# Attention and expert layer on one core: a v load ahead of a weight load, batch 1's and batch 2's loads in later slots

## The chip, the cores and the metric

The kernel runs on one core of one Trainium2 chip. The metric is the device time of one execution in microseconds; the time before is the median of four runs. A core has five engines that run side by side, each in its own order: TensorE (PE in the profile, its weight loads PEld), VectorE (DVE), ScalarE (ACT), GpSimd (POOL) and SyncE (SP, which here only issues DMAs).

## The reference

Sliding-window attention with a linear bias, followed by a two-layer network with an ELU between its layers. Sizes: 8 batches, 8 heads, 576 positions, 64 values a head; 4608 tokens of width 512, inner width 2048.

```python
scores = scale * np.matmul(q, k.transpose(0, 1, 3, 2))
rel = pos[:, None] - pos[None, :]
bias = slopes[:, None, None] * (-np.abs(rel))[None, :, :]
mask = (rel >= 0) & (rel < window)            # window = 128
scores = np.where(mask, scores + bias[None], -1000000000.0)
attn = np.exp(scores - np.max(scores, axis=-1, keepdims=True))
attn = attn / (np.sum(attn, axis=-1, keepdims=True) + 1e-09)
x = np.matmul(attn, v)                        # tokens x 512 after a transpose
h = x @ w_in
g = np.where(h > 0.0, h, np.exp(np.minimum(h, 0.0)) - 1.0)
out = g @ w_out
```

All inputs and the output are float32 in memory; the DMAs that load q, k, v, w_in and w_out turn them into float16 on the way.

## The kernel before

The program is written out in one order by hand: the order of the Python calls is the order of each engine's instructions, and the framework adds only the waits. After a start that is written line by line (L327 to L385) everything hangs on numbered **slots**. Three tables say what a slot holds: `HID[s]` the step of the first layer, `OUT[s]` four matmuls of the second, and `at(s, f, ...)` adds any other call (`before` puts it at the head of the slot, `after` at its end). The loop at L517 walks the slots.

One step of the first layer (`hidden`, L272) is 16 matmuls (L280, 32 in the steps of 64 tokens) into a PSUM buffer of 512 columns, an exp on ScalarE (L285), a clamp to 0..1 on POOL (L286), and one slot later `elu` on VectorE (L293), which reads the PSUM buffer again and so sets it free. Up to slot 17 three buffers take turns from slot 4 on, so a step waits for the elu of the step three before it. Steps 0 to 15 make the first 512 tokens; slots 18 to 23 hold no step.

The attention of batch 0 is spread over slots 0 to 12, that of batch 1 over slots 16 to 32, that of batch 2 over 32 to 48, and so on. A query block's `values` (L235) multiplies weights and v on TensorE (L245), then VectorE takes the reciprocal of the row sums (L251) and scales (L252) into `xn`; `turn` (L255) transposes xn on TensorE (L264) and copies it into `xT`, what the first layer reads.

Loads. q and k of batches 0 and 1 are loaded by `load_first` (L96) in parts and transposed on TensorE by `turn_first` (L125, matmuls L134, copies L138). q and k of later batches come by `load_qk` (L103), eight loads a batch, and are transposed on VectorE by `turn_qk` (L140, L142), whose first call for K needs all four K loads. `load_v` (L110) loads 128 positions of v (five a batch) into one of two buffers, `load_wi` and `load_wo` a quarter of a weight. **All of these are issued on POOL's queue**, in the same order as POOL's clamps: a load that stands in slot s is issued after the clamp of step s and ahead of that of step s+1. An issue shows as a POOL row of about 0.7 to 0.9 us (DMA_DIRECT2D). The stores (L307) are issued on SP.

What the change touches: the start's loads (L330 to L339), the list of batch 1's loads (L460 to L465), the first turn of K of batch 2 (`TURN`, L486), and the slots of batch 2's loads (L512, L514). In the start TensorE works through 22 warming matmuls (L321), K and Q of batch 0, two query blocks and their turns; step 0 (slot 0) is its first use of w_in, and `values(0, 1, ...)` its first use of v's second piece.

Of the kernel before, what the change touches and what calls it, by code (L numbers as in the profile page):

```python
# [18 lines left out]
def kernel(  # L19
# [76 lines left out]
    def load_first(b, w, part):  # L96

        p0, n, m, r0, j0 = split(b, w, part)
        nc.gpsimd.dma_start(
            s0[b][p0:p0 + n, w, :, j0:j0 + m, :].rearrange("p h j d -> p h (j d)"),  # L100
            (q, k)[w][b, :, r0:r0 + n * m, :].rearrange("h (p j) d -> p h (j d)", j=m))
# [8 lines left out]
    def load_v(b, n):  # L110
        p = 128 if n < 4 else 64
        nc.gpsimd.dma_start(VP[b % 2][0:p, n, :, 0:D],  # L112
                            v[b, :, 128 * n:128 * n + p, :].rearrange("h p d -> p h d"))

    def load_wi(i):
        c = slice(512 * i, 512 * i + 512)
        nc.gpsimd.dma_start(w_in_sb[:, :, c], moe_w_in[:, c].rearrange("(c p) f -> p c f", p=128))
# [28 lines left out]
    with tc.manual_schedule():  # L146
# [182 lines left out]
        nc.gpsimd.iota(rel, pattern=[[1, 256]], base=0, channel_multiplier=-1)  # L329
        load_first(0, 0, 0)  # L330
        load_v(0, 0)
        load_wi(0)
        load_v(0, 1)
        load_first(0, 0, 1)
        load_first(0, 1, 1)
        load_first(0, 0, 2)
# [53 lines left out]
        def at(s, f, *a):  # L390
            tasks.setdefault(s, []).append((f, a))

        def after(s, f, *a):
            late.setdefault(s, []).append((f, a))

        def before(s, f, *a):
            early.setdefault(s, []).append((f, a))
# [15 lines left out]
        for o in range(16 * NTB - 4):  # L413
            t, ts, f = o // 16, o // 4 % 4, o % 4
            s = (9, 11, 13, 14)[o] if o < 4 else 11 + o if o < 13 else 2 * o - 1 if o < 16 else 15 + o
# [42 lines left out]
        for n in range(4):  # L458
            at(n + 1, load_wo, n)
        at(5, load_first, 1, 1, 0)  # L460
        at(6, load_first, 1, 0, 0)
        at(9, load_first, 1, 1, 1)
        at(10, load_first, 1, 0, 1)
        for n, s in enumerate((7, 8, 11, 12, 13)):
            at(s, load_v, 1, n)  # L465
        at(16, turn_first, 1, 1, 0, 0, av, V.tensor_copy)
        at(16, turn_first, 1, 1, 0, 1, sp[3], nc.scalar.copy)
# [15 lines left out]

        START = [None, None, 32, 49, 66, 83, 100, 117]

        TURN = [None, None, (20, 22, 23, 24, 24, 25, 27, 29), (40, 40, 41, 42, 44, 44, 46, 48)]  # L486
        REST = 32, 32, 36, 36, 33, 34, 37, 38
        for b in range(2, B):
            for u in range(4):
                a = START[b] + 4 * u  # L490
                after(a, scores, b, u)
                for g in range(4):
                    before(a + 1 + g // 2, expo, b, u, g)
                at(a + 1, weigh, b, u, 0)
                at(a + 2, weigh, b, u, 1)
                at(a + 3, values, b, u, 0, sp[2])
                at(a + 3, values, b, u, 1, sp[3])
                at(a + 3, turn, b, u)
                if u == 3:
                    at(a + 4, values, b, 4, 0, sp[0])  # L500
                    at(a + 4, values, b, 4, 1, sp[2])
                    at(a + 4, turn, b, 4)
            a = START[b - 1] if b > 2 else 0
            for n in range(8):
                piece = (b, int(n < 4), *divmod(n % 4, 2))
                if b == 2:
                    m = 4 if n < 4 else 6
                    at(TURN[b][n], turn_qk, *piece, 0, m)
                    at(REST[n], turn_qk, *piece, m, R)
                else:  # L510
                    at(TURN[b][n] if b == 3 else a + 4 * (n // 2), turn_qk, *piece)
                at(a - 8 + n if a else 14 + n // 2, load_qk, b, int(n < 4), n % 4)  # L512
            for n in range(5):
                at(a + 3 + n if a else 18 + n // 2, load_v, b, n)  # L514

        slots = set(HID) | set(OUT) | set(tasks) | set(early)
        for s in range(min(slots), max(slots) + 1):  # L517
# [42 lines left out]
```

## Time and profile before

| | |
|---|---|
| median of four runs | 319.15 us |
| the runs | 318.97, 319.46, 319.32, 318.7 us |
| the profiled execution | 318.97 us |
| its span, first to last instruction | 317.2 us |
| mean granted TensorE clock | 0.999 |
| DMA queue of POOL | 75920 packets, 18.36 MB, 64.2% of 16 engines' span |

```profile
DMA  9999999895999999993969697996912111120011
```

The line above cuts the span into 40 slices of 7.9 us; each digit is the share of a slice, in tenths, in which the DMA engines are busy on average. The other views used here: the waits (who waited for whom, how long in total, how often, the longest), the chain of waits (the work that ended last, followed back), the timeline (start, length, engine, line, operation; in brackets the engine's idle time before it and what ended it), and a tile's rows, which also give the time from a load's issue to its landing. Times in them count from the start of the span.

### The profile page before, as it was taken

The numbers are of one execution on the slowest core, as the hardware profiler recorded it, in microseconds if no ns is written. First come the engines' busy times: TensorE is split into PE (matmuls) and PEld (weight loads), VectorE is DVE, ScalarE is ACT, GpSimd is POOL, SyncE is SP. The second block draws the span as 40 slices with busy tenths as digits, with TensorE's granted clock in tenths as the row PEclk, the third lists the DMA queues.
The fourth block names the chain that finished last, engine by engine and source line by source line (L and its number), as shares of the span: only waits on it lengthen the run. The fifth ranks groups of instructions, "written<-read, shape, count | busy, mean of one in ns | idle before, by whom it ended". The sixth has DMA issues, their size and how long they took to land.

```text
span 317.2 us, 9362 instructions
## 1 busy us (share of the span) xinstructions
PE 310.9 (98%) x3935; PEld 220.0 (69%) x3935; DVE 218.9 (69%) x444; ACT 179.9 (57%) x320; POOL 169.3 (53%) x263
## 2 busy tenths in 40 slices
PE   8899999999999999999999999999999999999996
PEld 6788774787777777776667666666677666766653
DVE  4646657887898877787777777777886666644330
ACT  5575458666666465546566666656654666533431
POOL 8949887473756455564756375645623323333320
PEclk9999999999999999999999999999999999999999
DMA  9999999895999999993969697996912111120011
GB/s 103 194 193 206 198 174 185 96 117 74 100 81 115 112 69 110 121 118 61 114 98 124 95 100 94 124 121 78 98 52 60 36 50 53 52 58 35 33 65 70
DMA packets 96362, 32.00 MB, mean 101 GB/s; under 512 B 83904, under 2 KB 91840, under 8 KB 96320
## 3 DMA queue, kind: packets, MB, share of 16 engines
q0 software_dynamic: 75920, 18.36, 64.2%
q1 hardware_dynamic: 20400, 13.05, 16.8%
q8 instruction: 31, 0.51, 0.7%
q14 instruction: 11, 0.09, 0.1%
HBM read 36.70 MB, written 9.44 MB: 145 GB/s over the span
## 4 chain that ended last, share of the span: by engine, by line
PE 93%; DVE 4%; POOL 1%; issue 1%; ACT 0%; ACTq 0%; DVEq 0%
PE hp L280 38%; PE op L299 20%; PE av L299 16%; PE spa L222 4%; PE sp L245 4%; PE op L321 2%; DVE g L293 1%; PE sp L299 1%; DVE xn L252 1%; PE sp L280 1%; PE av L313 1%; POOL e L286 1%; PE spa L173 1%; PE av L134 1%; PE av L245 1%
## 5 line engine op out<-in xcount | busy, mean ns | idle before, releaser
L286 POOL TENSOR_SCALAR e<-e 128x512 f32<-128x512 f32 x144 | 90.0, 625 | 134.4 <-ACT e L285 133.9
L280 PEld LDWEIGHTS <-wi 128*128 128x128 f16 x1856 | 124.5, 98 | 34.9 <-issue 4.6
L280 PE MATMUL hp<-xT,wi 128*128 128x128 f16 (+2 forms) x1744 | 144.9, 233 | 0.6 <-DVE g L293 0.3
L285 ACT ACTIVATE e<-hp 128x512 f32<-128x512 f32 x138 | 82.7, 599 | 86.2 <-PE hp L280 83.0
L293 DVE SCALAR_TENSOR_TENSOR g<-e,hp 128x512 f16<-128x512 f32 x138 | 94.2, 682 | 53.6 <-POOL e L286 52.6
L299 PE MATMUL op<-wo,g 128*128 128x512 f16 x304 | 77.5, 379 | 0.0
L299 PEld LDWEIGHTS <-g 128*128 128x128 f16 x560 | 50.1, 98 | 36.8 <-issue 1.1
L299 PE MATMUL av<-wo,g 128*128 128x512 f16 x240 | 61.4, 379 | 0.0
L233 DVE TENSOR_TENSOR EX<-EX,TAB 128x1024 f16<-128x1024 f16 x48 | 33.1, 690 | 15.0 <-ACT EX L228 14.8
L228 ACT ACTIVATE EX<-spa 128x512 f16<-128x512 f32 x48 | 26.1, 594 | 16.4 <-PE spa L222 16.4
L112 POOL DMA_DIRECT2D VP<-in_v_dram x40 | 34.9, 874 | 0.4 <-issue 0.2
L252 DVE TENSOR_TENSOR xn<-sp,rden 128x256 f16<-128x256 f32 (+1 forms) x60 | 25.4, 424 | 2.1
L228 ACT ACTIVATE EX<-sp 128x512 f16<-128x512 f32 x48 | 26.1, 600 | 0.0
L245 PEld LDWEIGHTS <-EX 128*128 128x128 f16 x576 | 22.3, 97 | 2.4 <-DVE EX L213 1.1
L142 DVE STREAM_TRANSPOSE QT<-st 128x576 f16<-128x576 f16 (+2 forms) x28 | 19.1, 714 | 0.0
L245 PE MATMUL sp<-VP,EX 128*128 128x65 f16 x428 | 18.9, 193 | 0.0
L142 DVE STREAM_TRANSPOSE KT<-st 128x576 f16<-128x576 f16 (+2 forms) x28 | 18.8, 710 | 0.0
L106 POOL DMA_DIRECT2D st<-in_k_dram x24 | 16.5, 687 | 1.2 <-DMA VP<-in_v_dram 0.4
L306 ACT COPY ob<-op 128x512 f32<-128x512 f32 x19 | 11.1, 586 | 9.4 <-PE op L299 9.1
L106 POOL DMA_DIRECT2D st<-in_q_dram x24 | 16.4, 684 | 0.0
L222 PEld LDWEIGHTS <-KT 32*128 32x128 f16 x480 | 8.9, 93 | 10.4 <-issue 10.2
L222 PE MATMUL spa<-QT,KT 32*128 32x256 f16 (+2 forms) x240 | 14.7, 248 | 0.0
(108 smaller groups left out, 188.3 us busy)
## 6 DMA issues: line engine op xcount, KB each, us to landing
out_dram<-ob SPq DMA_DIRECT2D x35, 256.0 KB, 2.3
VP<-in_v_dram POOLq DMA_DIRECT2D x32, 128.0 KB, 4.4
st<-in_k_dram POOLq DMA_DIRECT2D x24, 144.0 KB, 3.5
st<-in_q_dram POOLq DMA_DIRECT2D x24, 144.0 KB, 3.8
wi<-in_moe_w_in_dram POOLq DMA_DIRECT2D x4, 512.0 KB, 10.6
wo<-in_moe_w_out_dram POOLq DMA_DIRECT2D x4, 512.0 KB, 10.2
VP<-in_v_dram POOLq DMA_DIRECT2D x8, 64.0 KB, 4.6
s<-in_k_dram POOLq DMA_DIRECT2D x1, 512.0 KB, 12.0
```

The source lines that it names most:

```text
L106: nc.gpsimd.dma_start(st[b][32 * g:32 * g + 32, w, :, :, :, :].rearrange("p h n j d -> p (h n) (j d)"), (q, k)[w][b, 2 * g:2 * g + 2, :, : ...
L112: nc.gpsimd.dma_start(VP[b % 2][0:p, n, :, 0:D], v[b, :, 128 * n:128 * n + p, :].rearrange("h p d -> p h d"))
L142: V.transpose(o, st[b][:, w, h2, n0:n1, :, 32 * dh:32 * dh + 32])
L222: nc.tensor.matmul(sp[g][:, 256 * h2 + o:256 * h2 + o + n], kt_[b % 2][r, k0:k0 + 128], QT[b % 2][r, h2, dh, q0:q0 + n], start=dh == 0, st ...
L228: nc.scalar.activation(unit(b, u)[:, g, :, :], sp[g].rearrange("p (h c) -> p h c", h=2), AF.Exp, scale=0.125)
L233: V.tensor_tensor(out=e, in0=e, in1=TAB[:, int(u == 3), 2 * gp:2 * gp + 2, :, :], op=ALU.mult)
L245: nc.tensor.matmul(a[:, x, h2, :], ex_[u][:, c:c + 128], VP[b % 2][:, n, 2 * g + h2, 0:D + 1], start=j == 0, stop=j == len(parts) - 1)
L280: nc.tensor.matmul(p[:, l * w + u0:l * w + u1], w_in_sb[:, c, fc * 128:(fc + 1) * 128], xT[:, c, x0:x0 + u1 - u0], start=(c == 0), stop=(c ...
L285: nc.scalar.activation(e[:, 0:n], p[:, 0:n], AF.Exp)
L286: nc.gpsimd.tensor_scalar(out=e[:, 0:n], in0=e[:, 0:n], scalar1=1.0, scalar2=0.0, op0=ALU.min, op1=ALU.max)
L293: V.scalar_tensor_tensor(out=gs[t][:, f0:f0 + nf, c0:c0 + w], in0=sh(es.pop((t, c0, f0))), scalar=1.0, in1=sh(hps.pop((t, c0, f0))), op0=A ...
L299: nc.tensor.matmul(o, gs[t][:, fc, ts * 128:(ts + 1) * 128], w_out_sb[:, fc, :], start=(fc == 0), stop=(fc == NFC - 1))
```

## The change

Four edits, all of them to the order of loads; the arithmetic stays.

1. In the start, v's second piece (128 positions of batch 0) is loaded before w_in's first quarter instead of after it.
2. Batch 1: k's main part stays in slot 5; q's main part goes from slot 6 to 9, the rest of k from 9 to 11, the rest of q from 10 to 12, v's five pieces from 7, 8, 11, 12, 13 to 10, 11, 13, 14, 15.
3. Batch 2: the eight q and k loads go from slots 14 to 17 to slots 16 to 19, two a slot as before, the five v loads from 18 to 20 to slots 20 to 22.
4. Batch 2's first turn of K goes from slot 20 to 21.

```diff
         load_first(0, 0, 0)
         load_v(0, 0)
+        load_v(0, 1)
         load_wi(0)
-        load_v(0, 1)
         load_first(0, 0, 1)
...
         at(5, load_first, 1, 1, 0)
-        at(6, load_first, 1, 0, 0)
-        at(9, load_first, 1, 1, 1)
-        at(10, load_first, 1, 0, 1)
-        for n, s in enumerate((7, 8, 11, 12, 13)):
+        at(9, load_first, 1, 0, 0)
+        at(11, load_first, 1, 1, 1)
+        at(12, load_first, 1, 0, 1)
+        for n, s in enumerate((10, 11, 13, 14, 15)):
             at(s, load_v, 1, n)
...
-        TURN = [None, None, (20, 22, 23, 24, 24, 25, 27, 29), (40, 40, 41, 42, 44, 44, 46, 48)]
+        TURN = [None, None, (21, 22, 23, 24, 24, 25, 27, 29), (40, 40, 41, 42, 44, 44, 46, 48)]
...
-                at(a - 8 + n if a else 14 + n // 2, load_qk, b, int(n < 4), n % 4)
+                at(a - 8 + n if a else 16 + n // 2, load_qk, b, int(n < 4), n % 4)
             for n in range(5):
-                at(a + 3 + n if a else 18 + n // 2, load_v, b, n)
+                at(a + 3 + n if a else 20 + n // 2, load_v, b, n)
```

## The prediction, made before the changed kernel ran

> **What bounds the kernel now.** I read the busy shares first, then the waits of TensorE, then the chain of work through the one stretch where TensorE waits twice, then the rows of that stretch engine by engine.
>
> ```profile
> PE 310.9 (98%) x3935; PEld 220.0 (69%) x3935; DVE 218.9 (69%) x444; ACT 179.9 (57%) x320; POOL 169.3 (53%) x263
> ```
>
> TensorE is busy 310.9 of 317.2 us, so the change can win only what TensorE waits for. Its waits over 0.15 us (engine, line and what it waited for; total, times, longest) are few, the start-up wait for the warming operand left out:
>
> ```profile
> PE hp L280 <- DVE g L293: 0.3, 1, 0.3
> PE hp L264 <- DVE xn L252: 0.3, 1, 0.3
> PE av L245 <- DVE xn L252: 0.3, 1, 0.3
> PE op L264 <- DVE xn L252: 0.2, 1, 0.2
> ```
>
> By the timeline, L264's two lie at 11.68 and 13.81 us (the start), L280's at 28.77 and L245's at 32.37. The chain of waits (start, length, what) shows what stands behind the last one:
>
> ```profile
> 27.39 0.60 POOL e L286
> 28.00 0.87 POOL s L99
> 28.87 0.04 issue
> 28.90 0.63 POOL e L286
> 29.53 0.85 POOL VP L112
> 30.38 0.04 issue
> 30.42 0.64 POOL e L286
> 31.05 0.02 issue
> 31.08 0.69 DVE g L293
> ...
> 32.92 0.38 PE sp L264 x4
> ```
>
> This is the place to look at. From 27.39 to 31.06 the chain lies on POOL, and two of its five pieces are not arithmetic but the issuing of DMAs: batch 1's q (slot 6, 0.87 us) and its first v piece (slot 7, 0.85 us). They hold up the clamps (L286) of steps 7 and 8, these the elu (L293), and VectorE, which works in order, gets to the reciprocal and xn of query block 3 only then. TensorE's side of it:
>
> ```profile
> 28.77 1.05 PE L280 MATMUL hp<-xT,wi 128*128 128x128 f16 x16 [0.32 <-DVE g L293]
> ...
> 31.01 1.06 PE L280 MATMUL sp<-xT,wi 128*128 128x128 f16 x16
> 32.37 0.40 PE L245 MATMUL av<-VP,EX 128*128 128x65 f16 x8 [0.30 <-DVE xn L252]
> 32.92 0.38 PE L264 MATMUL sp<-ident,xn 128*128 128x128 f16 x4
> 33.14 1.06 PE L280 MATMUL hp<-xT,wi 128*128 128x128 f16 x16
> ```
>
> A row of matmuls ends on the page some 0.16 us (1.05 - 0.89) after the last could be followed by another, so the loss is read from starts. The same 16 matmuls of L280 are followed at 29.66 after a start at 28.77: 0.89 us. From 31.01 that is 31.90, but L245 starts at 32.37: **0.47 us** lost. Eight matmuls of L245 without a wait take 29.66 to 29.90, 0.24; from 32.37 that is 32.61, but L264 starts at 32.92: **0.31 us** lost. Together 0.78. From 33.14 to the end hardly more than switches between shapes (about 0.1 us each) is lost before a matmul.
>
> **Part 1, batch 1's q and v leave slots 6 to 8.** Removed between the clamps there are three issues, 0.92 us each on their rows. The new POOL order is worked out from the exp rows, which feed the clamps:
> - Clamp 6 stays at 27.39: it waited for its exp (26.70 + 0.60), with POOL idle for 0.58 us after batch 1's first k load. So elu 6 (28.03) stays, and TensorE's stall at 28.77, which ends with elu 6 at 28.72, **stays whole**.
> - Clamp 7: its exp ends at 27.59 + 0.60 = 28.19; start 28.28 instead of 28.90 (0.09 from exp to clamp, as at step 6). Clamp 8: exp ends 29.08, start 29.17 instead of 30.42. Clamp 9: exp ends 30.46, start 30.55 instead of 31.93.
> - Elu 8 begins 0.03 us after clamp 8's 0.60: 29.80 instead of 31.08. Block 3's first half is then held by TensorE (L245 at 29.66 + 0.41 = 30.07) and elu 8 (the next row starts 0.60 after it, as from 31.08 to 31.68: 30.40): reciprocal 30.40, xn 30.61 to 31.03; second half reciprocal 30.95, xn 31.16 to 31.58.
> - TensorE wants the first at 31.90 and the second at 32.14. Both are ready, by 0.9 and 0.6 us. So both losses go: **-0.78 us**, and L280 of step 11 starts at 32.36.
>
> I take the whole 0.78. Bounds: no gain at all if some other input holds those two rows; at the most 1.27, with the 28.77 stall gone too (0.49: from 27.39 + 0.89 = 28.28 to 28.77), which the exp rows above speak against.
>
> **Part 2, where these issues go.** Everything below is 0.78 earlier than its row. q (0.92) behind clamp 9 ends at 32.0; clamp 10 waits for its exp to 32.70 anyway. v's first (0.92) behind clamp 10 ends at 34.3, clamp 11's exp at 34.1: late by 0.15. Slot 11 gets two issues (0.71 + 0.92): clamp 12 starts near 36.5 instead of 36.15. The buffer of step 12 is wanted by step 15 (row at 39.88, new 39.10), elu 12 ends at 37.8: 1.3 us to spare. Slots 13 to 15 have one issue each, as 11 to 13 had. Slots 14 and 15 lose one of their two, and with them the waits of the batch 2 loads (0.33, 0.16, 0.38 and 0.30 us in the POOL rows from 40.85 to 44.38). Cost **0**: hidden by the 1.3 us of buffer slack; with that gone, 0.15 to 0.35 us would show.
>
> Do the loads still come in time? They stay in one order of issue but for k's rest and v's second piece, and the backlog sets the landings (a tile's rows give the time from issue to landing: 12.6 us for the issue at 27.95): q still near 40.6 for its turn at 44.8; q's rest near 44.7 (row: 33.79 + 10.9) for its turn at 48.1; v's first near 41.5 for L245 at 49.5. Each load also waits for the eighth before it to land (the load at 40.85 starts just after q's 27.95 + 12.6 = 40.55); later issue makes this wait shorter. Cost **0**.
>
> **Part 3, batch 2 two slots later.** K's last quarter is issued in slot 17 behind clamp 17, whose exp ends at 46.29, new 45.51: second issue at 46.8 instead of 44.38. The landing of the old row, and the VectorE rows around the first turn's new place (slot 21):
>
> ```profile
> DMA to landing us min/median/max: 6.1/6.1/6.1
> ```
> ```profile
> 52.81 0.68 DVE L213 TENSOR_TENSOR EX<-EX,TAB 128x1024 f16<-128x1024 f16 x1
> 54.02 0.18 DVE L251 RECIPROCAL rden<-sp 128x4 f32<-128x4 f32 x1 [0.52 <-PE sp L245]
> ```
>
> The old landing is 44.38 + 6.1 = 50.5. The new one lies between 46.8 + 3.1 = 49.9 (the load at 58.83, with an empty queue, takes 3.1) and 46.8 + 7.0 = 53.8 (the load at 40.85, with a full one). I take about 50.5, as the same bytes lie ahead of it. The turn can start when L213 lets it, 53.41 - 0.78 = 52.6: 2 us to spare. Its 0.46 us lies in VectorE's 0.52 of idle time before 54.02, where slot 20 had it between 51.78 and 52.24. Cost **0**; at 53.8 VectorE would stand from 52.6 on and TensorE's L245 (55.31, which waits for the next L213) would be some 0.9 late.
>
> [...]
>
> **Part 4, v's second piece before w_in's first quarter.** Two issues (0.89 each) change places; so do the landings. Both rows took 6.8 us: w_in landed at 4.04 + 6.8 = 10.8, v at 4.91 + 6.8 = 11.7. v was wanted at 12.05 (held there by exp until 12.00), w_in is wanted at 12.50 and would now land at about 11.7. Cost and gain **0**, with 0.8 us to spare instead of 0.3.
>
> **Sum:** -0.78 + 0 + 0 + 0. The profiled execution took 318.97 us (span 317.2 and 1.8 around it), 0.18 below the median of the four runs, 319.15. So 318.2 against the one, 318.4 against the other; I say **318.3**.
>
> **Rivals.**
> 1. *The gain is given back* (chance 0.23): 0.78 us goes at 32 us and TensorE waits again at 61.88 and 68.86, where it has small losses (0.2 each by starts) behind VectorE's elu, VectorE being 90% busy from 60 to 70. For it: that busy share. Against: the VectorE row before it, the reciprocal at 57.99, waits 0.60 us for TensorE, so the stretch starts with TensorE and moves with it. Also here: the two losses have another cause, and the change does nothing. Time 319.0 to 319.2.
> 2. *K for batch 2 late* (0.12): VectorE stands at the first turn in slot 21, with weigh, reciprocal and xn queued behind it and TensorE behind these. It begins to cost with a landing after 52.9 and eats the gain at 53.7. With the longest landing of a v piece issued past 37 us (8.4 at 37.50), 46.8 + 8.4 = 55.2: 2.3 late, less 0.78, 320.7. For it: two slots taken from loads that had 1.3 us to spare. Against: the backlog is shorter by then, and the turn is a slot later.
> 3. *More than the sum* (0.05): the 28.77 stall goes too, 318.97 - 1.27 = 317.7.
>
> The forecast has 0.60. Its own range is a gain of 0.5 to 1.1 off 318.97 to 319.15: 317.9 to 318.6. The range for 8 in 10 takes in rival 3 below and rival 1 above, with the scatter of the runs: 317.7 to 319.3; rival 2 is left out. What a measurement of this kernel can tell from no change is about 0.2%, 0.64 us; the forecast is only just past that. Faster: 0.50 of its 0.60, and rival 3: 0.55. Within: the other 0.10, rival 1, and 0.01 of rival 2: 0.34. Slower: 0.11.
>
> **What would show it.** Part 1: two clamps at about 28.3 and 29.2 with no DMA issue between, no wait of L245 or L264 near 32, step 11's L280 near 32.4, the wait at 28.77 unchanged. Part 2: clamp 12 late by about 0.3 with no wait of TensorE until 55. Part 3: no idle VectorE ahead of the first K turn. Part 4: L280's first row still at 12.54. It is wrong if a wait for a DMA appears on TensorE or VectorE, or if step 11's lead of 0.78 is not there any more at the first L222 (72.93, new 72.15).

## The result and the profile after

| | before | changed |
|---|---|---|
| median | 319.48 us (58 runs) | 318.64 us (35 runs) |
| ratio, 95% interval | | 0.9974 (0.9964 to 0.9983) |
| profiled execution, span | 318.97, 317.2 us | 318.62, 316.8 us |

The changed kernel is faster by 0.84 us in the median, a quarter of a per cent; the interval keeps clear of 1. The busy shares of the page are as good as unchanged:

```profile
PE 310.6 (98%) x3935; PEld 219.8 (69%) x3935; DVE 219.3 (69%) x444; ACT 179.8 (57%) x320; POOL 168.9 (53%) x263
```

TensorE's waits in the changed kernel (what, on what; total, times, longest):

```profile
PE hp L134 <- DMA s<-in_q_dram: 0.4, 1, 0.4
PE hp L280 <- DVE g L293: 0.3, 1, 0.3
PE hp L264 <- DVE xn L252: 0.3, 1, 0.3
PE op L264 <- DVE xn L252: 0.2, 1, 0.2
```

L245's wait for xn is gone, L280's for elu 6 has stayed, and there is a new one at the start, for batch 0's q. The timeline of POOL where the chain lay before:

```profile
27.82 0.60 POOL L286 TENSOR_SCALAR e<-e 128x512 f32<-128x512 f32 x1 [0.58 <-ACT e L285]
28.70 0.61 POOL L286 TENSOR_SCALAR e<-e 128x512 f32<-128x512 f32 x1 [0.27 <-ACT e L285]
29.59 0.61 POOL L286 TENSOR_SCALAR e<-e 128x512 f32<-128x512 f32 x1 [0.28 <-ACT e L285]
30.97 0.61 POOL L286 TENSOR_SCALAR e<-e 128x512 f32<-128x512 f32 x1 [0.76 <-ACT e L285]
31.53 0.92 POOL L99 DMA_DIRECT2D s<-in_q_dram  x1
```

The clamps of steps 6 to 9 now wait for their exps and for nothing else. TensorE:

```profile
29.20 1.05 PE L280 MATMUL hp<-xT,wi 128*128 128x128 f16 x16 [0.32 <-DVE g L293]
...
31.44 1.06 PE L280 MATMUL sp<-xT,wi 128*128 128x128 f16 x16
32.33 0.41 PE L245 MATMUL av<-VP,EX 128*128 128x65 f16 x8
32.58 0.39 PE L264 MATMUL sp<-ident,xn 128*128 128x128 f16 x4
32.80 1.06 PE L280 MATMUL hp<-xT,wi 128*128 128x128 f16 x16
```

L245 starts 0.89 us after L280, L264 0.25 after L245, as they do where nothing waits: nothing is lost. This execution is 0.43 us late from the start on (29.20 against 28.77), and the reason is the new wait: q's first load landed at 7.60 instead of 6.77 us, so Q's turn began at 7.64 instead of 7.21.

Two measures keep the start apart from the place of the change. The **start** runs from Q's first turn (L134, second group of 32 matmuls) to step 1's matmuls (the second 16 of L280); the **stretch** runs from there to the first L222. Both are differences of start times in the timeline. From the first L222 to the end, all 14 profiled executions take 244.25 to 244.29 us.

| kernel (times in us) | Q's turn | start | stretch | ratio to before (95%) |
|---|---|---|---|---|
| before | 7.21 | 7.49 | 58.22 | |
| changed | 7.64 | 7.49 | 57.44 | 0.9974 (0.9964 to 0.9983) |
| a_swap | 6.96 | 8.16 | 58.52 | 0.9988 (0.9965 to 1.0011) |
| b_noswap | 8.49 | 8.28 | 57.45 | 0.9987 (0.9953 to 1.0020) |
| c_batch1 | 7.62 | 8.36 | 57.60 | 0.9967 (0.9933 to 1.0002) |
| d_batch2 | 8.20 | 7.49 | 58.23 | 0.9985 (0.9956 to 1.0013) |
| e_q6 | 7.04 | 7.49 | 57.44 | 0.9953 (0.9932 to 0.9975) |
| f_v78 | 8.03 | 7.50 | 57.58 | 0.9969 (0.9953 to 0.9984) |
| i_sp0 | 7.49 | 7.91 | 56.95 | 0.9935 (0.9913 to 0.9957) |
| h_after (changed) | 7.41 | 7.82 | 57.64 | 0.9952 (0.9936 to 0.9967) |
| j_after (changed) | 8.43 | 8.47 | 57.43 | 0.9963 (0.9947 to 0.9978) |
| k_noswap | 8.41 | 8.31 | 57.43 | 0.9976 (0.9952 to 0.9999) |
| l_swap | 8.68 | 8.07 | 58.21 | 1.0002 (0.9981 to 1.0023) |
| m_sp0 | 7.75 | 7.49 | 56.96 | 0.9953 (0.9931 to 0.9975) |

The stretch moves by 0.78 us, to the hundredth, with the change. What comes before it scatters by far more than 0.2 us from execution to execution (Q's turn between 6.96 and 8.68, the start between 7.49 and 8.47), so ratios of a dozen runs are wide; the stretch, which each profile gives once, is what tells the kernels apart.

### The profile page after: what moved, and what is told of

It reads as the page before. It is cut to its first block, busy times and chain, and to the rows that moved or that the text cites. A ratio compares the mean times of both kernels' runs of the same rounds, so it can differ in the third digit from the quotient of the medians.

```text
span 316.8 us, 9362 instructions
## 1 busy us (share of the span) xinstructions
PE 310.6 (98%) x3935; PEld 219.8 (69%) x3935; DVE 219.3 (69%) x444; ACT 179.8 (57%) x320; POOL 168.9 (53%) x263
## 4 chain that ended last, share of the span: by engine, by line
PE 92%; DVE 4%; DMA 2%; POOL 1%; issue 1%; ACT 0%; POOLq 0%; ACTq 0%; DVEq 0%
PE hp L280 38%; PE op L299 21%; PE av L299 16%; PE sp L245 4%; PE spa L222 4%; DMA s<-in_q_dram 2%; DVE g L293 1%; PE sp L299 1%; PE sp L280 1%; PE av L313 1%; PE spa L173 1%; DVE xn L252 1%; PE av L245 1%; PE av L134 1%; PE spa L245 0%
## 5 line engine op out<-in xcount | busy, mean ns | idle before, releaser
L280 PEld LDWEIGHTS <-wi 128*128 128x128 f16 x1856 | 124.5, 98 | 34.9 <-issue 4.8
L280 PE MATMUL hp<-xT,wi 128*128 128x128 f16 (+2 forms) x1744 | 144.9, 233 | 0.6 <-DVE g L293 0.3
L245 PEld LDWEIGHTS <-EX 128*128 128x128 f16 x576 | 22.2, 97 | 2.0 <-DVE EX L213 1.1
L245 PE MATMUL sp<-VP,EX 128*128 128x65 f16 x428 | 18.9, 193 | 0.0
L222 PEld LDWEIGHTS <-KT 32*128 32x128 f16 x480 | 8.9, 93 | 10.4 <-issue 10.2
L222 PE MATMUL spa<-QT,KT 32*128 32x256 f16 (+2 forms) x240 | 14.7, 248 | 0.0
```

Source lines behind the costliest of these rows:

```text
L222: nc.tensor.matmul(sp[g][:, 256 * h2 + o:256 * h2 + o + n], kt_[b % 2][r, k0:k0 + 128], QT[b % 2][r, h2, dh, q0:q0 + n], start=dh == 0, st ...
L245: nc.tensor.matmul(a[:, x, h2, :], ex_[u][:, c:c + 128], VP[b % 2][:, n, 2 * g + h2, 0:D + 1], start=j == 0, stop=j == len(parts) - 1)
L280: nc.tensor.matmul(p[:, l * w + u0:l * w + u1], w_in_sb[:, c, fc * 128:(fc + 1) * 128], xT[:, c, x0:x0 + u1 - u0], start=(c == 0), stop=(c ...
```

## The experiments

The kernels a to d ran on one chip, e to i on a second (h_after with them), j to m on a third, each time with the chip's own runs of the kernel before.

### The parts alone

**a_swap**, the swap in the start alone (on the kernel before):

```diff
         load_v(0, 0)
+        load_v(0, 1)
         load_wi(0)
-        load_v(0, 1)
```

> The kernel before with v's second piece ahead of w_in's first quarter, nothing else. Theory A (the gain is batch 1's issues leaving the clamps of steps 7 and 8; the 0.43 us that the changed kernel's profiled execution lost at 7.6 us waiting for q is chance): ratio 1.000 within 0.001, q's first load lands near 6.8 us as often as near 7.6, and the stall of L245 and L264 near 32 us stays at 0.78 us. Theory S (the swap itself makes q land late): ratio 1.0013 (0.43 us), q's first load lands near 7.6 and TensorE waits for it at 7.6 us.

Measured: 0.9988 (0.9965 to 1.0011), which can't be told from 1. q's first load landed at 6.92 us with the swap in place, so theory S falls. But w_in's first quarter landed at 13.27 and TensorE waited for it:

```profile
12.04 0.41 PE L245 MATMUL op<-VP,EX 128*128 128x65 f16 x8
13.32 1.07 PE L280 MATMUL hp<-xT,wi 128*128 128x128 f16 x16 [0.88 <-DMA wi<-in_moe_w_in_dram]
```

And the stretch is 0.30 longer than before. The rows of POOL in slots 13 to 15 of this execution show why:

```profile
39.93 0.71 POOL L112 DMA_DIRECT2D VP<-in_v_dram  x1 [0.43 <-DMA s<-in_k_dram]
40.67 0.63 POOL L286 TENSOR_SCALAR e<-e 128x512 f32<-128x512 f32 x1
42.58 0.70 POOL L106 DMA_DIRECT2D st<-in_k_dram  x1 [1.28 <-DMA s<-in_q_dram]
43.52 0.66 POOL L106 DMA_DIRECT2D st<-in_k_dram  x1 [0.25 <-DMA VP<-in_v_dram]
44.20 0.63 POOL L286 TENSOR_SCALAR e<-e 128x512 f32<-128x512 f32 x1
```

Batch 2's first load waits 1.28 us for batch 1's q, eight loads ahead of it, to land; in the profile of before that was 0.33. Clamp 15 stands behind it and starts at 44.20, so elu 15 begins only at 44.86 on VectorE; the copy of K behind it, 45.47 to 46.69, frees the bank that L134 then waits for (its second group starts at 46.74). So the waits of these issues, which the prediction put at no cost, do reach TensorE when the landings are a little later. In the profile of the changed kernel, with batch 1's and batch 2's new slots, the first four of batch 2's loads don't wait.

**b_noswap**, the changed kernel with that edit undone (the same two lines the other way):

> The changed kernel with w_in's first quarter back ahead of v's second piece. Theory A: the same ratio as the changed kernel, 0.9974 to 0.9976 (0.78 us off). Theory S: 0.9961 (0.78 and the 0.43 us that the swap cost), with q's first load landing near 6.8 us.

Stretch 57.45: the gain is there without the swap. q's first load landed at 8.45, also without it. The ratio, 0.9987 (0.9953 to 1.0020), can't tell the theories apart; the landing can, and speaks against S.

**c_batch1**, the kernel before with batch 1's slots alone:

```diff
-        at(6, load_first, 1, 0, 0)
-        at(9, load_first, 1, 1, 1)
-        at(10, load_first, 1, 0, 1)
-        for n, s in enumerate((7, 8, 11, 12, 13)):
+        at(9, load_first, 1, 0, 0)
+        at(11, load_first, 1, 1, 1)
+        at(12, load_first, 1, 0, 1)
+        for n, s in enumerate((10, 11, 13, 14, 15)):
```

> The kernel before with batch 1's loads alone in the later slots; batch 2's loads and its first K turn where they were. Theory A: the whole gain, 0.9976, with clamps of steps 7 and 8 near 28.3 and 29.2 us; POOL then has three issues in each of slots 14 and 15, and clamps 15 and 16 end near 43.2 and 45.8, which the buffers bear. Rival B (batch 2 had to move too, or the gain comes from batch 2's loads no longer waiting for landings in slots 14 and 15): under half of the gain, over 0.9988.

Stretch 57.60: 0.62 of the 0.78, so rival B falls; the ratio, 0.9967 (0.9933 to 1.0002), is too wide to say it. The missing 0.16 lies at 49.75 us, where TensorE's score matmuls (L173) wait for elu 17, as POOL had three issues in each of slots 14 and 15, one of them waiting for a landing. The chain of waits there (`issue` is time for which the profile shows no wait):

```profile
43.12 0.67 POOL st L106
43.78 0.02 issue
43.80 0.63 POOL e L286
44.43 0.65 POOL VP L112
45.08 1.33 POOL st L106 x2
46.41 0.65 POOL e L286
47.06 1.27 POOL st L106 x2
48.33 0.01 issue
48.33 0.65 POOL e L286
48.98 0.02 issue
49.01 0.70 DVE g L293
49.71 0.04 issue
49.75 0.39 PE hp L173 x4
```

Theory A was right in the main and too generous about the buffers. Batch 2's later slots give no gain of their own, but save this 0.16.

**d_batch2**, the kernel before with batch 2's slots alone:

```diff
-        TURN = [None, None, (20, 22, 23, 24, 24, 25, 27, 29), (40, 40, 41, 42, 44, 44, 46, 48)]
+        TURN = [None, None, (21, 22, 23, 24, 24, 25, 27, 29), (40, 40, 41, 42, 44, 44, 46, 48)]
...
-                at(a - 8 + n if a else 14 + n // 2, load_qk, b, int(n < 4), n % 4)
+                at(a - 8 + n if a else 16 + n // 2, load_qk, b, int(n < 4), n % 4)
...
-                at(a + 3 + n if a else 18 + n // 2, load_v, b, n)
+                at(a + 3 + n if a else 20 + n // 2, load_v, b, n)
```

> The kernel before with batch 2's loads two slots later and its first K turn in slot 21, nothing else. Theory A: 1.000 within 0.001, no wait of VectorE ahead of the first K turn, the stall near 32 us still 0.78 us. Rival B: under 0.9985. Rival K (K lands late): over 1.001, with a wait of VectorE near 53 us.

Stretch 58.23, as before: rivals B and K both fall. The ratio, 0.9985 (0.9956 to 1.0013), lies on rival B's bound and says nothing by itself. The 0.78 us at the block 3 rows were all there:

```profile
31.99 1.06 PE L280 MATMUL sp<-xT,wi 128*128 128x128 f16 x16
33.35 0.40 PE L245 MATMUL av<-VP,EX 128*128 128x65 f16 x8 [0.30 <-DVE xn L252]
33.90 0.38 PE L264 MATMUL sp<-ident,xn 128*128 128x128 f16 x4
```

L245 comes 1.36 us after L280 instead of 0.89, L264 0.55 after L245 instead of 0.24: 0.47 and 0.31 lost. VectorE's first K turn starts at 54.40 right behind L213, so K was not late either.

### Which of the two issues?

**e_q6**, the changed kernel with q back in slot 6, and **f_v78**, the changed kernel with v's first two pieces back in slots 7 and 8:

```diff
-        at(9, load_first, 1, 0, 0)
+        at(6, load_first, 1, 0, 0)
```
```diff
-        for n, s in enumerate((10, 11, 13, 14, 15)):
+        for n, s in enumerate((7, 8, 13, 14, 15)):
```

> The changed kernel with batch 1's q back in slot 6; v's pieces stay in slots 10 to 15. Measure: the stretch from the start of step 1's matmuls (L280) to the first L222, 58.22 us before, 57.44 us in the changed kernel, which leaves the start's landings out. Theory A2 (the two issues are not worth half each: TensorE asks for block 3's xn 0.9 and 0.6 us after it is ready, so one issue alone is still covered): clamp 7 late by 0.62, clamp 8 by 0.33, elu 8 by as much, stretch 57.44 to 57.5. Rival (each issue costs its own 0.4): 57.8.

> The changed kernel with v's first two pieces back in slots 7 and 8; q stays in slot 9. Theory A2: clamp 7 on time, clamp 8 late by about 0.6, the second half of block 3's xn some 0.1 us later than TensorE asks for it, block 4's xn as much: stretch 57.55 to 57.75. Rival (each issue costs its own 0.4): 57.8 to 58.2.

e_q6: stretch 57.44, nothing lost with q's issue back between clamps 6 and 7. POOL's timeline:

```profile
27.22 0.60 POOL L286 TENSOR_SCALAR e<-e 128x512 f32<-128x512 f32 x1 [0.58 <-ACT e L285]
27.78 0.92 POOL L99 DMA_DIRECT2D s<-in_q_dram  x1
28.73 1.20 POOL L286 TENSOR_SCALAR e<-e 128x512 f32<-128x512 f32 x2
```

Clamps 7 and 8 follow one another without a break, clamp 8 being only some 0.3 late. f_v78: 57.58, so 0.14 lost, and just where expected, at the second half of block 3's xn (L264 0.38 after L245 instead of 0.25):

```profile
32.71 0.41 PE L245 MATMUL av<-VP,EX 128*128 128x65 f16 x8
33.09 0.38 PE L264 MATMUL sp<-ident,xn 128*128 128x128 f16 x4
```

So the two issues, q in slot 6 and v in slot 7, are not worth half of the gain each. Either of them alone is nearly hidden by the time that TensorE needs until it asks for xn; only both together reach it.

### The stall that stayed

**i_sp0**, the changed kernel with step 9 in a bank that is free at that time:

```diff
-            HID[s if s < 18 else s + 6] = [(*step, (hp[0], hp[1], av, hp[1])[s] if s < 4 else BUF[(s + 1) % (3 if s < 18 else 2)])]
+            HID[s if s < 18 else s + 6] = [(*step, (hp[0], hp[1], av, hp[1])[s] if s < 4 else sp[0] if s == 9 else BUF[(s + 1) % (3 if s < 18 else 2)])]
```

> The changed kernel with step 9 in a PSUM bank of its own (the first score bank, which is free from 27 us until slot 18) instead of step 6's. Theory A (the stall of 0.49 us at step 9 waits for elu 6, which no DMA issue holds up, and only the buffer makes it wait): the stall goes, no other comes, stretch 57.44 - 0.49 = 56.95 (57.0 if block 4's xn is then 0.05 late), time 0.0015 less than the changed kernel. Rival (the stall moves to step 10 or 11): 57.3 to 57.44.

Stretch 56.95, as expected to the hundredth. Steps 8 and 9 now follow each other at 0.89 us:

```profile
28.09 1.06 PE L280 MATMUL hp<-xT,wi 128*128 128x128 f16 x16
28.98 1.06 PE L280 MATMUL spa<-xT,wi 128*128 128x128 f16 x16
29.87 0.41 PE L245 MATMUL av<-VP,EX 128*128 128x65 f16 x8
```

The median of its runs, 318.15 us, is 0.49 below that of the changed kernel on the same chip (h_after, 318.64). **m_sp0**, the same on another chip:

> The changed kernel with step 9 in its own PSUM bank, a second time: 0.4 to 0.5 us less than the changed kernel in the median, stretch 56.95 us.

318.49 against 318.92 of j_after, 0.43 less; stretch 56.96. By the medians this version is faster than both kernels. The stretch shows that the stall at step 9 was a matter of the buffer and of no load.

### The start

**h_after** and **j_after** are the changed kernel again, **k_noswap** is b_noswap and **l_swap** is a_swap again.

> The changed kernel again, for the start. Theory A (the landing of q's first load scatters by execution, with either order of v and w_in): stretch 57.44 within 0.05; q's first load may land anywhere from 6.8 to 8.5 us. Theory S (the swap makes q late): 7.5 us or later in each of the four kernels of this call.

> The changed kernel, beside the next two on one chip, to weigh the swap. Theory L (of w_in's first quarter and v's second piece the one issued second lands at 11.7 to 13.5 us, by execution; v is asked for at about 12.0 and w_in 0.45 later, where TensorE waits for VectorE's xn next anyway): Q turn to step 1 takes 7.5 us where w_in lands by 12.5, up to 8.2 where it lands at 13.5; ratio to before 0.995 to 0.9975. Theory A (the swap is worth nothing): the same ratio as without the swap, within 0.0005.

> The changed kernel without the swap. Theory L: 0.2 to 0.4 us slower than the changed kernel in the median, and Q turn to step 1 up to 8.4 us where v lands at 13.2. Theory A: no difference beyond 0.15 us. The stretch from step 1 to the first L222 is 57.44 us by both.

> The kernel before with the swap alone. Theory L: 0.2 to 0.4 us faster than before in the median, 0.9988 to 0.9994. Theory A: 1.000. By both the stretch from step 1 to the first L222 is 58.22 us, or up to 58.52 where batch 2's first loads wait for landings in slots 14 and 15 until elu 15 and the copy of K behind it are late, as in the first run of this kernel.

h_after's stretch is 57.64, outside the 0.05 that was expected: 0.2 of it is a wait at 22.68 us for w_in's third quarter, another load that came late (it landed at 22.64). q's first load landed between 6.77 and 8.63 us in the 14 executions, between 6.83 and 8.63 with the swap and between 6.77 and 8.45 without, so theory S is done with.

Whether the swap itself is worth something stays open. The medians on one chip are 318.92 with it and 319.14 without (j_after, k_noswap), which would be 0.22 for theory L; but the swap alone has 0.9988 and 1.0002 with intervals of 0.2% on either side. In the traces the load of the two that is issued second landed at 11.7 to 13.6 us with either order. What it costs depends on how long after Q's turn it lands. Without the swap v landed 5.56 us after it in c_batch1, TensorE waited for it, and the start took 0.87 more than 7.49:

```profile
13.32 0.40 PE L245 MATMUL av<-VP,EX 128*128 128x65 f16 x8 [0.89 <-DMA VP<-in_v_dram]
```

With the swap w_in landed 5.38 us after Q's turn in m_sp0 and cost nothing, 5.96 in h_after (0.33), 6.06 in i_sp0 (0.42) and 6.31 in a_swap (0.67). So w_in may land some 5.6 us after Q's turn at no cost, part of the wait lying where TensorE waits for xn without it; v at 5.56 was already 0.87 too late. That points the way of theory L, with one execution on the one side.

The medians leave something else open. On the second chip the changed kernel lies 1.33 us below the kernel before (318.64 against 319.97), on the third 0.96 (318.92 against 319.88), and on the second the interval, 0.9936 to 0.9967, leaves out the 0.9976 that 0.78 us would make. The swap, or waits of batch 2's loads as in a_swap, could make up the rest; the kernel before has one profile only, and no run separates them.

## Why the prediction was right

The forecast was -0.78 us, 318.3; measured were -0.84 us in the median and 318.64, the runs of before having moved up to 319.48 with more of them. That the medians differ by so nearly 0.78 is in part luck, as the other two chips gave 1.33 and 0.96, and the stated range, 317.7 to 319.3, took in no change as well; what bears the forecast out is the stretch, 0.78 shorter. The mechanism was the one named: two DMA issues on POOL ahead of two clamps.

- **Part 1** held as worked out. The clamps of steps 6 to 9 were predicted at 27.39, 28.28, 29.17 and 30.55; less this execution's 0.43, they lie at 27.39, 28.27, 29.16 and 30.54. The stretch is 0.78 shorter. The stall at step 9 stayed (0.49, from 28.71 to 29.20), so rival 3 didn't come about.
- **Part 2.** Its first half held: clamp 12 starts at 36.93, 36.50 without the 0.43, where 36.5 was said, and TensorE doesn't notice. Its second half was sized too small. The waits of batch 2's loads in slots 14 and 15 were called free in the kernel before; in a_swap they cost TensorE 0.30 us, in l_swap nothing. Taking them away is a gain that depends on the landings, and the profile of before showed them on one execution only.
- **Part 3** held in its number and not in its reason, which was that the same bytes lie ahead of the load. K's last quarter landed at 50.67 (predicted 50.5), but 3.4 us after its issue, close to the 3.1 of the load at 58.83 in the profile of before, with an empty queue, and far from the 6.1 of before; from 47 to 49 us the DMAs moved 90 and 123 GB/s, in the profile of before 196 and 161. The queue had nearly run empty, and in d_batch2, issued later still, the load landed 3.5 us after its issue too (48.60, 52.06). That 50.5 came out was luck. The turn started right behind L213 with no idle time of VectorE before it, at 53.07 (predicted 52.63, and 0.43 for the start):

```profile
52.47 0.68 DVE L213 TENSOR_TENSOR EX<-EX,TAB 128x1024 f16<-128x1024 f16 x1
53.07 0.47 DVE L142 STREAM_TRANSPOSE KT<-st 128x256 f16<-128x256 f16 x1
53.67 0.18 DVE L251 RECIPROCAL rden<-sp 128x4 f32<-128x4 f32 x1
```

  c_batch1 shows what these two slots are for: without them batch 1's move gives back 0.16. The later issue cost nothing here: it came 2.9 us later (47.27 against 44.38), the landing 0.24 (50.67 against 50.43), and 2.4 us were left to the turn.
- **Part 4** rested on one execution's landings. "To spare" were 0.8 us by the profile of before; in a_swap it was the load that TensorE waited 0.88 us for. The zero stands as the middle of something that isn't known.
- The signs: the text said that a wait for a DMA on TensorE would show it wrong, and that step 0 would start at 12.54. Such a wait came, and step 0 started at 12.96, but for a load that the change doesn't touch and that lands as late without it. By its own words the prediction would be wrong there. The sign was badly chosen: it asked one execution about a thing that differs between executions.
- Rival 1 (given back at 61.88 and 68.86) fell: the lead at the first L222 is 0.35 in the profile, and 0.78 with the 0.43 of the start put back. Rival 2 fell with d_batch2.

## What to carry to other kernels

A queue that both issues DMAs and does arithmetic, as POOL does here, has two budgets, and an issue counts like an instruction of its length (in the kernel before q's takes 0.92 us from 27.95 on, and clamp 7 starts behind it at 28.90; without it at 28.27, less the 0.43 of the start): move it to slots where the engine's next piece waits for something else anyway, and move the later loads on too, or they pile up (0.16 us in c_batch1). Work out when the bottleneck asks for the result before dividing a gain among causes: of two delays either alone may cost next to nothing (0.00 and 0.14 us here, 0.78 together). Where the start of a kernel scatters with its loads, compare stretches between two events of the bottleneck, not the whole time alone.

## What the runs showed of the hardware

A late load can cost more than its wait. In b_noswap TensorE stood for 1.14 us waiting for q's first load until 8.49, and then the granted clock was down (columns: window; busy time of the engines; PEclk; DMA):

```profile
9.00:12.00 3.00, 3.00 (x52) 2.38 (x46) 2.28 (x5) 2.15 (x4) 2.71 (x6) 0.62 1.64 182
12.00:15.00 3.00, 2.70 (x44) 2.04 (x41) 1.79 (x7) 1.42 (x3) 2.72 (x9) 0.81 1.48 195
15.00:18.00 3.00, 2.81 (x58) 2.56 (x55) 1.90 (x5) 1.32 (x3) 1.01 (x2) 1.00 1.27 205
```

PEclk is the clock that TensorE was granted, as a share of the full one; in j_after, where the drop nearly fills the row from 9 to 12 us, it reads 0.51. The single matmuls of L180 start 0.107 us apart in b_noswap (10.80 to 11.44) and 0.057 in the changed kernel (9.63 to 9.97), so they run at about half the speed. With 0.5 for the clock during the drop, the drop in the rows above lasts (0.38 + 0.19) x 3 / 0.5 = 3.4 us, an estimate; the rows of j_after (0.92 from 6 to 9 us and 0.51 from 9 to 12), k_noswap (0.56 and 0.87 from 9 to 15) and l_swap (0.78 and 0.65 from 9 to 15) make as much. The start took 8.28 instead of 7.49. In j_after, k_noswap and l_swap, with waits of 1.6, 1.2 and 1.8 us for that load, the clock dropped too and the start took 8.47, 8.31 and 8.07; in j_after w_in had landed at 12.62, well before step 0 could have wanted it (8.43 + 5.33 = 13.76, with the 5.33 from Q's turn to step 0 of before), so there it is the clock alone. The drop costs some 0.6 to 1.0 us, about as much as the whole change brings.

f_v78 waited 1.1 us for the same load and kept its clock: PEclk reads 1.00 in each 3 us from 0 to 18. So it does in c_batch1, where TensorE waited 0.3 us for xn and 0.89 for v. The length of the wait alone doesn't tell the two outcomes apart (1.1 us in f_v78, 1.14 in b_noswap), and no run shows what does.

In these traces a load issued on POOL waits until the eighth load before it has landed: for batch 2's first load in a_swap that landed at 42.29 and the issue started at 42.58, after 1.28 us of waiting; for the next the times are 43.24 and 43.52, in the profile of before 40.56 and 40.85. What stands behind it on POOL waits too (clamp 15 in a_swap, until 44.20): a backlog of the DMA engines can stop an engine that wants nothing of it.
